# A windowed-attention and token-MLP kernel: gate factors spread on VectorE, two independent last evictions, layer norm on two engines, and a new plan

## The chip, the core and the metric

The kernel runs on one core of one Trainium2 chip. A core has TensorE (matmul), VectorE (DVE in the profile), ScalarE (ACT), GpSimd (POOL) and SyncE (SP), which here only issues DMAs. Each engine works through its own list of instructions in order, and semaphores tie the lists together. The metric is the device time of one launch in microseconds (us); lower is better.

## What is computed

```python
x = A_x                                   # 1 x 2048 x 512, bf16
g = sigmoid((x * gate_w).sum(-1))         # one gate per token
# a: 32 heads of 16, causal, each query sees its last 256 keys
q, k, v = split_heads(x @ wqkv)
p = softmax(where(0 <= i - j < 256, q @ k.T * 16**-0.5, -1e9))
a = (p @ v) @ wo
# b: an MLP over the 2048 tokens, for each of the 512 columns
h = layernorm(x)                          # over the 512 columns
u = gelu(einsum("sd,sf->df", h, w1) + b1)     # f = 1376
b = einsum("df,fs->sd", u, w2) + b2
out = g * a + (1 - g) * b
```

## The kernel before

Tokens lie in 16 tiles of 128, and in four blocks of four tiles. Everything stays in SBUF; x, the weights and the output pass DRAM once.

**Start.** x arrives in tiles `xo`; two blocks are transposed on TensorE (L702) and two by transposing DMAs (L579) into `XT`. While x and the weights arrive, TensorE does projections (L740): keys to `KT`, queries to `QZ` (L794, each query once with the even and once with the odd heads zeroed), values to `VA`, each followed by an eviction from PSUM by VectorE or ScalarE. SP's queue takes the loads in order of priority; the copies `VS` of the values with swapped halves (L774, L775) go through it too.

**Attention** goes by groups of queries that lie half a tile off the token tiles. For each group there are score matmuls (L985, and L965 for the two half tiles at the window's ends), exponentials on ScalarE (L1010, two of 128x1024 each), masks on VectorE (L1026, L1043) or GpSimd (L639), and value matmuls (L1069). VectorE then transposes 32x32 blocks, takes the reciprocal of the sum, multiplies (L1131 to L1148) and transposes back into `xo` (L1166). In L1139 the reciprocal is multiplied by exp(x . gate_w), which lies in `EZ`.

**The gate.** TensorE makes x . gate_w as a column, one token per partition (L841); VectorE limits it (L854), ScalarE takes the exponential into `ez` (L860). At L1139, though, tokens lie 32 to a partition group: `EZ` must hold in every one of the four groups of 32 partitions the factors of all four. So GpSimd splits the fp32 factor into three bf16 parts (four instructions, L866 to L869), TensorE multiplies them by four 0/1 matrices `spread` (twelve matmuls of 4 columns, L876), and VectorE or ScalarE copies the 128x16 result from PSUM to `EZ` (L885). This happens four times, once for a block.

**Layer norm.** VectorE makes the statistics (L810, L814), GpSimd one over the root of the variance (L820, L821), VectorE the normalised tile `h` (L826, 16 of them).

**The MLP.** Eleven chains u of 16 matmuls over the tokens (L740, `h` times w1 in `wb`), each waiting for all 16 tiles of `h` and for its column group of w1 (three groups, loaded in four pieces each); after the last u one gelu on ScalarE. Then w2 is loaded over w1, and 16 chains y of 15 matmuls follow, 11 from the MLP and 4 from the attention with `wo`; the bank of each is evicted by VectorE (L551) or ScalarE (L548) as c1 * y + c2 into `ot`, which is stored. The last tile is evicted in two halves of 256 columns, `f15.0` and `f15.256`, and stored once.

**The order.** `arrange` is a planner inside the program. Every task names its engine or engines with a cost, what it depends on, and a priority, which is a base from `ORDER` plus an offset by name from `SHIFT`. The planner builds the lists of all engines: the next task is one that can start earliest; among those that can start within `patience` of each other the lowest priority wins. For TensorE a change between dense matmuls (mode "d") and the tiled ones of attention adds `stick` to the priority, a change between two attention modes adds `join`. A task with two engines is offered to both. `two=True` marks VectorE instructions that share an SBUF port with GpSimd; the planner keeps those apart from GpSimd's work, and a wait is put in where a GpSimd task follows within 1 us. `Task` objects are then emitted in the planned order. For PSUM, whose tiles alias, the program itself adds a wait for whoever used the bank before, if that was another engine: readers too.

```python
pw = add(f"pow{i}", {"POOL": 1.6}, power, ag + [k0], 5)
hready.append(add(f"h{t_}", {"DVE": 0.41}, emit_h, [pw], ORDER["ln"] - 0.5 + i, two=True))
...
b, t = chain(f"u{fc}", mms, dw1[g] + hready, ORDER["u"] + ORDER["u_step"] * fc, "u")
...
gready = add("gates", {"DVE": 0.45}, gates, eready + [k3, m1[4]], 30, two=True)
```

## Time and profile before

| | |
|---|---|
| median of 3 runs | 216.52 us (214.58 to 216.78) |
| the profiled execution | 215.1 us, its span 213.4 us |
| TensorE busy | 203.0 us, 95% of the span, 3723 matmuls |
| ScalarE, VectorE, GpSimd busy | 169.0, 154.1, 56.8 us |
| matmuls of the spread, L876 | 48, in groups of 12 at 25.4, in 30 to 35 (two), and at 75.2 us |
| h tiles, L826 | 16 on VectorE, 16.1 to 57.7 us, 406 ns each |
| first matmul on h | 57.9 us |
| last matmul ends | 209.4 us |
| granted TensorE clock | 1.00 throughout |

The span goes from the first to the last instruction; the time of the execution has 1.7 us more around it. The profile's "busy" of TensorE counts modelled ends of pipelined matmuls, so 100% busy means that no gap shows, not that the array does its peak. In the chain that ended last each piece is what released the next one; a piece of TensorE with x12 stands for twelve matmuls in a row.

### The profile page before, as it was taken

The numbers are of one execution on the slowest core, as the hardware profiler recorded it, in microseconds if no ns is written. First come the engines' busy times: TensorE is split into PE (matmuls) and PEld (weight loads), VectorE is DVE, ScalarE is ACT, GpSimd is POOL, SyncE is SP. The second block draws the span as 40 slices with busy tenths as digits, with TensorE's granted clock in tenths as the row PEclk, the third lists the DMA queues.
The fourth block names the chain that finished last, engine by engine and source line by source line (L and its number), as shares of the span: only waits on it lengthen the run. The fifth ranks groups of instructions, "written<-read, shape, count | busy, mean of one in ns | idle before, by whom it ended". The sixth has DMA issues, their size and how long they took to land.

```text
span 213.4 us, 8309 instructions
## 1 busy us (share of the span) xinstructions
PE 203.0 (95%) x3723; PEld 93.6 (44%) x3723; DVE 154.1 (72%) x248; ACT 169.0 (79%) x196; POOL 56.8 (27%) x78
## 2 busy tenths in 40 slices
PE   7999998988999999999999999999999999999992
PEld 3444433432444454544554345453354445345550
DVE  1786899999988757675766768377666778537872
ACT  3164899989999789979787999778989697987721
POOL 8720422495029722021222240202230202003000
PEclk9999999999999999999999999999999999999999
DMA  4999976955330000000190693010110010000002
GB/s 145 333 181 79 281 242 198 303 199 135 82 82 3 3 3 3 3 3 0 29 367 6 213 394 78 5 54 0 59 35 3 28 49 28 28 25 28 31 3 74
DMA packets 24867, 20.34 MB, mean 95 GB/s; under 512 B 8864, under 2 KB 23200, under 8 KB 24832
## 3 DMA queue, kind: packets, MB, share of 16 engines
q1 hardware_dynamic: 21328, 19.80, 30.7%
q0 software_dynamic: 3504, 0.01, 3.0%
q8 instruction: 29, 0.48, 1.0%
q14 instruction: 6, 0.05, 0.1%
HBM read 15.47 MB, written 2.10 MB: 82 GB/s over the span
## 4 chain that ended last, share of the span: by engine, by line
PE 81%; ACT 8%; DVE 6%; DMA 2%; issue 1%; SPq 1%; ACTq 0%; DVEq 0%
PE pb L740 58%; PE ps L1069 11%; PE ps L985 8%; ACT et L1010 5%; PE ps L965 2%; DMA wqkv<-in_A_wqkv_dram 2%; DVE QZ L794 1%; DVE h L826 1%; ACT VA L693 1%; ACT KT L693 1%; DVE VA L694 1%; PE pb L841 1%; DVE ps L1131 1%; ACT XT L1010 1%; DVE XT L1026 1%
## 5 line engine op out<-in xcount | busy, mean ns | idle before, releaser
L1010 ACT ACTIVATE et<-ps 128x1024 bf16<-128x1024 f32 (+1 forms) x108 | 101.6, 1002 | 15.0 <-PE ps L985 11.4
L1010 ACT ACTIVATE XT<-ps 128x1024 bf16<-128x1024 f32 (+1 forms) x46 | 43.7, 1004 | 7.3 <-PE ps L985 3.8
L639 POOL TENSOR_SCALAR_AFFINE_SELECT et<-et 128x1024 bf16<-128x1024 bf16 (+1 forms) x26 | 30.2, 1162 | 64.6 <-ACT et L1010 45.6
L740 PEld LDWEIGHTS <-wb 128*128 128x128 bf16 (+2 forms) x352 | 30.8, 99 | 37.3 <-issue 6.0
L740 PE MATMUL pb<-h,wb 128*128 128x512 bf16 (+1 forms) x176 | 43.4, 381 | 0.0
L740 PE MATMUL pb<-ug,wb 128*128 128x512 bf16 (+1 forms) x176 | 42.8, 380 | 0.0
L740 PE MATMUL pb<-XT,wqkv 128*128 128x512 bf16 x128 | 32.3, 380 | 1.0 <-DMA wqkv<-in_A_wqkv_dram 0.4
L1131 DVE STREAM_TRANSPOSE ps<-ps 128x1024 f32<-128x1024 f32 (+1 forms) x17 | 20.4, 1197 | 8.0 <-PE ps L1069 7.9
L985 PE MATMUL ps<-QZ,KT 32*128 32x256 bf16 (+1 forms) x528 | 24.0, 262 | 2.1 <-ACT XT L1010 0.7
L1069 PEld LDWEIGHTS <-VA 128*32 128x32 bf16 (+1 forms) x1472 | 21.8, 94 | 9.6 <-issue 5.0
L639 POOL TENSOR_SCALAR_AFFINE_SELECT XT<-XT 128x1024 bf16<-128x1024 bf16 x9 | 10.3, 1145 | 56.1 <-ACT XT L1010 38.3
L794 DVE TENSOR_TENSOR QZ<-pb,par 128x1024 bf16<-128x1024 f32 x16 | 19.4, 1218 | 3.8 <-PE pb L740 3.6
L1043 DVE TENSOR_TENSOR et<-et,mask 128x1024 bf16<-128x1024 bf16 (+1 forms) x20 | 15.3, 764 | 9.2 <-ACT et L1010 9.1
L1069 PE MATMUL ps<-et,VA 128*32 128x128 bf16 (+2 forms) x1024 | 20.2, 211 | 0.0
L985 PEld LDWEIGHTS <-KT 32*128 32x128 bf16 x528 | 8.0, 92 | 24.7 <-ACT et L1010 11.2
L551 DVE TENSOR_SCALAR ot<-pb,c,c 128x512 bf16<-128x512 f32 (+1 forms) x14 | 11.0, 787 | 9.4 <-PE pb L740 9.4
L740 PE MATMUL pb<-wqkv,XT 128*128 128x512 bf16 x64 | 16.7, 381 | 0.9 <-ACT VA L693 0.5
L740 PE MATMUL pb<-wo,xo 128*128 128x512 bf16 x64 | 17.0, 380 | 0.0
L740 PEld LDWEIGHTS <-wqkv 128*128 128x128 bf16 x128 | 10.7, 97 | 14.2 <-ACT VA L693 1.2
L1166 DVE STREAM_TRANSPOSE xo<-zt 128x512 bf16<-128x512 bf16 (+1 forms) x17 | 11.5, 678 | 0.4
L550 DVE TENSOR_SCALAR ug<-pb,b1c 128x512 bf16<-128x512 f32 (+1 forms) x10 | 7.5, 751 | 5.7 <-PE pb L740 5.7
L1148 DVE TENSOR_TENSOR zt<-ps,rd 128x512 bf16<-128x512 f32 (+1 forms) x17 | 11.2, 657 | 0.5
(70 smaller groups left out, 178.9 us busy)
## 6 DMA issues: line engine op xcount, KB each, us to landing
wb<-in_B_w_dram SPq DMA_DIRECT2D x8, 512.0 KB, 6.6
wb<-in_B_w_dram SPq DMA_DIRECT2D x2, 2048.0 KB, 8.6
out_dram<-ot SPq DMA_DIRECT2D x16, 128.0 KB, 1.7
xo<-in_A_x_dram SPq DMA_DIRECT2D x3, 512.0 KB, 6.6
wb<-in_B_w_dram SPq DMA_DIRECT2D x4, 352.0 KB, 5.1
VS<-VA SPq DMA_DIRECT2D x32, 36.0 KB, 3.0
wqkv<-in_A_wqkv_dram SPq DMA_DIRECT2D x4, 256.0 KB, 5.2
wb<-in_B_w_dram SPq DMA_DIRECT2D x1, 1024.0 KB, 6.4
```

The costliest lines, as they stand in the source:

```text
L550: return nc.vector.tensor_scalar(out=out_, in0=in_, scalar1=bias, scalar2=None, op0=ALU.add)
L551: return nc.vector.tensor_scalar(out=out_, in0=in_, scalar1=scale, scalar2=bias, op0=ALU.mult, op1=ALU.add)
L639: return nc.gpsimd.affine_select(out=out_, in_=in_, pattern=[[0, n] for n in pattern] + [[step, HB]], compare_op=op, fill=0.0, base=base_, ...
L740: nc.tensor.matmul(buf(b)[:rows, :], lhsT=lhsT, rhs=rhs, start=(j == 0), stop=(j == n - 1))
L794: lambda k=k, b=b: nc.vector.tensor_tensor(out=QZ[:, k, :, (i % NQ) * SB:(i % NQ + 1) * SB], in0=buf(b)[:, None, :].to_broadcast([P, 2, SB ...
L985: made.append(nc.tensor.matmul(to[:, :, done:done + m], lhsT=keys(t_, k)[rows], rhs=q[rows], start=True, stop=True, tile_position=(32 * r, 0),
L1010: lambda n_=n_: nc.scalar.activation(out=shape(buf(e)[:, n_ * 1024:(n_ + 1) * 1024]), in_=shape(buf(b2[n_])), func=ACT.Exp, scale=SCALE),
L1043: return nc.vector.tensor_tensor(out=view, in0=view, in1=mask[:, "AB".index(x), None, :].to_broadcast([P, n_, HB]), op=ALU.mult)
L1069: return lambda: nc.tensor.matmul(to(), lhsT=v, rhs=buf(e)[rows, col:col + n], start=first, stop=last, tile_position=(rows.start, 32 * r), ...
L1131: f"n1{j}", {"DVE": 0.10 + 0.53 * f_}, lambda: nc.vector.transpose(out=view(), in_=view()), [last], 1, uses=[o],
L1148: lambda: nc.vector.tensor_tensor(out=buf(zt)[:, 0:w].rearrange("q (k b d) -> q k b d", k=4, d=DH), in0=blocks_of()[:, :, :, 0:DH], in1=bu ...
L1166: return nc.vector.transpose(out=to, in_=src)
```

## The change

Four things, and a new plan:

- The spread of the gate factors goes from GpSimd, TensorE and an eviction to VectorE alone: seven `tensor_copy` a block in fp32, four of 32x4 that bring the four partition groups of `ez` into the first group of `EZ`, and three of 32x16 that copy the first group to the others. `spread`, `z3`, `zr`, the sixteen GpSimd instructions, the 48 matmuls and the PSUM bank they used go.
- The evictions of y are marked `reads=True`. A task so marked waits for those who wrote the bank, and no longer for another such reader on another engine. It matters where two evictions read one bank, that is for the last tile.
- `h` can be made on GpSimd as well; the planner chooses.
- `lead`, `patience`, `stick`, `join`, `aside` and all offsets in `SHIFT` are new, so the order on every engine and in SP's queue is new.

```diff
 
 class Task:
     def __init__(self, name, engines, emit, deps=(), prio=50.0, lat=None, takes=(), uses=(), after=(), mode="d",
-                 two=False, ins=0):
+                 two=False, ins=0, reads=False):
         self.name = name
         self.engines = dict(engines)
         self.emit = emit
...
         self.two = two
 
         self.ins = ins
+
+        self.reads = reads
         self.takes = list(takes)
         self.uses = list(uses)
         for b in self.takes + self.uses:
...
 ORDER = dict(
     k=250.875, q=17.921, v=613.443, u=80.631, u_step=68.7, y=341.56, a=-49.601, pv=-51.223, s=-4.599,
-    gate=15.0, lead=-0.617, block=245.251, patience=0.326, m=-229.1, ln=1183.669, ev=255.775,
-    gelu=0.0, w1=71.797, pt=-57.398, stick=4.2, join=-164.3, aside=0.479, vs=2.0, wv=0.547, x=10.235,
+    gate=15.0, lead=-19.522, block=245.251, patience=0.215, m=-229.1, ln=1183.669, ev=255.775,
+    gelu=0.0, w1=71.797, pt=-57.398, stick=-171.7, join=-1591.5, aside=0.438, vs=2.0, wv=0.547, x=10.235,
     x_step=0.571, xt=11.397, xt_step=8.828,
 )
 BANKS = dict(
...
 ]
 
 SHIFT = {
...
-    "x1.4": -1901.8, "x2.8": -2292.5, "x3.12": -735.1, "xt2": -1707.8, "xt3": 662.4, "w1_00": -427.5,
...
-    "pow0": -18.0, "h0": -1266.0, "h1": -2653.7, "h2": -3891.3, "h3": -1642.6, "bs4": -1278.3, "ba4": -1289.3,
...
-    "h12": -1329.9, "h13": -1997.3, "h14": -1889.7, "h15": -1409.0, "gate0": -372.7, "gatem0": -1479.4,
...
-    "y15.10": 3400.9, "y15.11": 3855.9, "y15.13": 3855.8, "f15.0": -2180.0, "f15.256": -824.9, "o15": -1228.7,
...
+    "wv": -2289.8, "x1.4": -2247.8, "x2.8": -1082.1, "x3.12": 964.7, "xt2": -312.8, "xt3": 2434.4, "w1_00": 1746.3,
...
+    "h0": 546.5, "h1": 546.9, "h2": 627.3, "h3": 533.1, "bs4": -3903.9, "ba4": -151.4, "bs5": -4513.9,
...
+    "ba14": 528.7, "bs15": 416.3, "ba15": 389.6, "pow3": 2073.8, "h12": 818.2, "h13": -231.1, "h14": 3402.0,
...
+    "y15.13": 7360.2, "f15.0": -2153.2, "f15.256": -1705.3, "o15": 5622.7,
...
 }
...
     ez = sb.tile([P, NT], FP32, name="ez")
 
     EZ = sb.tile([P, 4 * NT], FP32, name="EZ")
-    z3 = sb.tile([P, 3, NT], BF16, name="z3")
-    zr = sb.tile([P, NT], FP32, name="zr")
     zeros = ug[:, 0, :]
     ident = sb.tile([P, P], BF16, name="ident")
-    spread = sb.tile([P, 4, P], BF16, name="spread")
     mask = sb.tile([P, 6, HB], BF16, name="mask")
     par = sb.tile([P, 2], FP32, name="par")
     gwc = sb.tile([P, 4], BF16, name="gwc")
...
         nc.gpsimd.memset(VA[:, :, H * DV:], 1.0)
 
     k5 = add("ones", {"POOL": 2.8}, ones, prio=3)
-
-    k7 = add(
-        "spread", {"ACT": 0.62},
-        lambda: nc.scalar.activation(
-            spread[:].rearrange("p a (r m) -> p a r m", r=4),
-            ident[:].rearrange("p (a m) -> p a m", m=32)[:, :, None, :].to_broadcast([P, 4, 4, 32]), ACT.Copy,
-        ),
-        [k1], prio=4,
-    )
 
     add("table", {"ACT": 1.4}, lambda: nc.scalar.activation(th[:], eps[:, 0:1], ACT.Exp), [k0], prio=0)
...
         pw = add(f"pow{i}", {"POOL": 1.6}, power, ag + [k0], 5)
         for t_ in range(4 * i, 4 * i + 4):
             def emit_h(t_=t_):
-                return nc.vector.tensor_scalar(
+                return (nc.vector if engine[0] == "DVE" else nc.gpsimd).tensor_scalar(
                     out=h[:, t_, :], in0=xo[:, t_, :], scalar1=mv[:, t_, 0:1], scalar2=rstd[:, t_:t_ + 1],
                     op0=ALU.subtract, op1=ALU.mult,
                 )
-            hready.append(add(f"h{t_}", {"DVE": 0.41}, emit_h, [pw], ORDER["ln"] - 0.5 + i, two=True))
+            hready.append(add(f"h{t_}", {"DVE": 0.41, "POOL": 0.8}, emit_h, [pw], ORDER["ln"] - 0.5 + i, two=True))
...
         )
         eready.append(ge)
 
-        def thirds(ts=ts):
-
-            nc.gpsimd.tensor_copy(out=z3[:, 0, ts], in_=ez[:, ts])
-            nc.gpsimd.tensor_tensor(out=zr[:, ts], in0=ez[:, ts], in1=z3[:, 0, ts], op=ALU.subtract)
-            nc.gpsimd.tensor_copy(out=z3[:, 1, ts], in_=zr[:, ts])
-            nc.gpsimd.tensor_tensor(out=z3[:, 2, ts], in0=zr[:, ts], in1=z3[:, 1, ts], op=ALU.subtract)
-
-        gs = add(f"third{i}", {"POOL": 3.7}, thirds, [ge], 3)
-        zb = bank("xt")
-
-        def pick(zb=zb, ts=ts):
-            return [
-                nc.tensor.matmul(
-                    buf(zb)[:, 4 * a:4 * a + 4], lhsT=spread[:, a, :], rhs=z3[:, m, ts], start=(m == 0), stop=(m == 2),
-                )
-                for a in range(4) for m in range(3)
-            ]
-
-        zp = add(f"pick{i}", {"PE": 0.35}, pick, [gs, k7], 3, takes=[zb], ins=24)
-        zready.append(add(
-            f"picked{i}", {"DVE": 0.2, "ACT": 0.25},
-            lambda zb=zb, i=i: (nc.scalar.copy if engine[0] == "ACT" else nc.vector.tensor_copy)(
-                out=EZ[:, 16 * i:16 * i + 16].rearrange("p (t a) -> p a t", a=4),
-                in_=buf(zb)[:, 0:16].rearrange("p (a t) -> p a t", t=4),
-            ),
-            [zp], 3, uses=[zb],
-        ))
+        def emit_spread(ts=ts, i=i):
+
+            to = EZ[:, 16 * i:16 * i + 16].rearrange("p (t a) -> p a t", a=4)
+            made = [nc.vector.tensor_copy(out=to[0:32, a], in_=ez[32 * a:32 * a + 32, ts]) for a in range(4)]
+            for r in range(1, 4):
+                made.append(nc.vector.tensor_copy(
+                    out=EZ[32 * r:32 * r + 32, 16 * i:16 * i + 16], in_=EZ[0:32, 16 * i:16 * i + 16]
+                ))
+            return made
+
+        zready.append(add(f"ez{i}", {"DVE": 0.9}, emit_spread, [ge], 3))
...
                 lambda b=b, ot=ot, t_=t_, c0=c0, c1_=c1_: affine(
                     buf(ot)[:, c0:c1_], buf(b)[:, c0:c1_], c1[:, t_:t_ + 1], c2[:, t_:t_ + 1]
                 ),
-                [t, gready], 2, takes=[] if c0 else [ot], uses=[b, ot] if c0 else [b],
+                [t, gready], 2, takes=[] if c0 else [ot], uses=[b, ot] if c0 else [b], reads=True,
             )
             for c0, c1_ in cols
         ]
...
                 if b.ring is not ps:
                     continue
                 for i in range(b.index, b.index + b.size):
-                    for who, ins in last[i]:
-                        if who != t.engine:
+                    for who, ins, reads in last[i]:
+                        if who != t.engine and not (reads and t.reads):
                             tc.add_manual_dep(
                                 first, ins.name,
                                 mybir.DependencyInfo(mybir.DependencyClass.Sync, mybir.DependencyReason.DATA),
                                 reason="psum bank",
                             )
-                    last[i] = [(t.engine, final)]
+                    last[i] = (last[i] if t.reads else []) + [(t.engine, final, t.reads)]
```

## The prediction

> **What bounds the kernel now.** I read the page's first part, then busy time by stretches, the chain that ended last, and the timeline at the places the change touches. The first line is busy time by engine. The others are stretches: limits, length, then busy us and (instructions) of PE, PEld, DVE, ACT, POOL, then granted clock, DMA share, GB/s.
>
> ```profile
> PE 203.0 (95%) x3723; PEld 93.6 (44%) x3723; DVE 154.1 (72%) x248; ACT 169.0 (79%) x196; POOL 56.8 (27%) x78
> ...
> 20.00:30.00 10.00, 9.76 (x110) 4.26 (x107) 8.50 (x17) 7.51 (x14) 3.42 (x13) 1.00 0.97 283
> 30.00:40.00 10.00, 8.69 (x211) 3.80 (x212) 9.49 (x20) 9.96 (x16) 3.39 (x3) 1.00 0.67 194
> 40.00:50.00 10.00, 8.72 (x153) 3.55 (x152) 9.54 (x22) 9.27 (x13) 6.84 (x10) 1.00 0.64 204
> 50.00:57.90 7.90, 7.15 (x200) 2.94 (x198) 7.51 (x18) 7.89 (x10) 1.31 (x2) 1.00 0.48 105
> 57.90:209.40 151.50, 150.87 (x2964) 70.44 (x2956) 106.91 (x149) 125.83 (x133) 32.01 (x31) 1.00 0.17 57
> ```
>
> Two regimes. From 57.9, where the first u matmul starts, to 209.4 TensorE idles 0.63 us of 151.5: only less TensorE work shortens that. From 20 to 57.9 it idles 0.24 + 1.31 + 1.28 + 0.75 = 3.58 us, while VectorE is busy 35.0 of 37.9 us and ScalarE 34.6: these two hold TensorE back, and TensorE has nothing else to do, as every u chain waits for all sixteen h tiles. The clock is full throughout.
>
> Four pieces of the chain (start, length):
>
> ```profile
> 25.45 0.45 PE pb L876 x12
> ...
> 75.07 0.28 PE pb L876 x12
> ...
> 209.43 0.56 DVE ot L551
> 210.01 0.56 ACT ot L548
> ```
>
> and from the timeline of VectorE and GpSimd:
>
> ```profile
> 21.19 0.16 DVE L854 TENSOR_SCALAR ez<-pb 128x4 f32<-128x4 f32 x1 [0.61 <-PE pb L841]
> 21.27 0.40 DVE L826 TENSOR_SCALAR h<-xo,mv,rstd 128x512 bf16<-128x512 bf16 x1
> ...
> 50.35 1.99 DVE L826 TENSOR_SCALAR h<-xo,mv,rstd 128x512 bf16<-128x512 bf16 x6
> ...
> 55.71 2.02 DVE L826 TENSOR_SCALAR h<-xo,mv,rstd 128x512 bf16<-128x512 bf16 x6
> ...
> 66.29 1.62 DVE L1043 TENSOR_TENSOR et<-et,mask 128x1024 bf16<-128x1024 bf16 x1
> ...
> 74.55 0.17 DVE L1214 TENSOR_SCALAR c<-ez 128x16 f32<-128x16 f32 x1
> 74.75 0.25 DVE L1215 RECIPROCAL c<-c 128x16 f32<-128x16 f32 x1
> 75.03 0.18 DVE L1216 TENSOR_TENSOR c<-c,b2c 128x16 f32<-128x16 f32 x1
> ...
> 0.80 2.28 POOL L663 MEMSET VA<- 128x512 bf16 x1 [0.29 <-POOLq L1304]
> ...
> 49.02 1.15 POOL L639 TENSOR_SCALAR_AFFINE_SELECT et<-et 128x1024 bf16<-128x1024 bf16 x1 [0.22 <-ACT et L1010]
> ```
>
> **The tail.** The two halves of the last tile run one after the other, 0.54 us on VectorE, then 0.56 us on ScalarE, with the last matmul done at 209.4. Without the wait both start there and the store leaves after the longer one: 210.57 becomes about 210.02, so **-0.55 us**, all on the path. What comes late next is the store, unchanged. Bounds: 0 (both halves on one engine) and -0.55. The Trainium skill speaks against this edit ("PSUM — Partial Sum Buffer", section "PSUM bank collisions raise a hardware error"): two engines that read one bank and quadrant at once collide, also at disjoint columns, and nothing is stalled. The trace shows no such overlap; by the rule the time would still fall by 0.55 and the data would be in danger, by the trace alone it falls by 0.55.
>
> **The gate spread, what goes.** 48 matmuls in four groups. Three (0.45 us each, from 25.4 to 33) lie where ScalarE and VectorE bind, and save nothing by themselves. The fourth at 75.07 lies in the full stage: 0.28, plus the break it makes in a dense run. A break costs about 0.1: in the chain two L740 matmuls take 0.54 and twelve 2.70, so 0.216 each and 0.11 over. I take **-0.38**; bounds -0.28 and -0.38. On ScalarE two copies of 0.20 go at 27 and 34, on VectorE one of 0.19 at 32; the 0.63 us at 3.83 lies in ScalarE's idle time. GpSimd loses sixteen small instructions, hidden.
>
> **The gate spread, what comes.** Seven dependent or neighbouring VectorE copies a group, 4 or 16 elements wide. No row shows a copy from one partition group to another. Below: 0.08 us from start to start, as from L854 to the next instruction, 0.56 for seven. Above: 0.28, as from L1215 to L1216, 2.0 for seven. The nearest row is L1214 with 0.17, so 1.2 for seven. Three groups fall before 57.9: 3.6 us on a full VectorE (1.7 to 6.0). The fourth falls where VectorE idles 45 us, and costs nothing; its factors are first used dozens of us later. The skill ("VectorE: DVE Perf Modes", section "Two Vector instructions with no wait between them") has a rule against it: an instruction whose start quadrant differs from the one before is held until that is done, so seven would take seven whole durations, 1.2 by L1214's row; without it, 0.6. What queues behind the copies is VectorE's in-order list, evictions for which TensorE and ScalarE wait.
>
> **h on GpSimd.** The new offsets of h are -231 to 3402 (before -3891 to -1266), so it yields to nearly everything, and goes where an engine is idle: GpSimd, 15 us busy of 37.9. An h costs VectorE 0.33 (1.99 / 6). If all fifteen after 20 us go, VectorE gets 5.0 us back; if none, 0. Its price on GpSimd no row shows: half a select is 0.57 (1024 elements take 1.15), the scattered memset of 512 elements 2.28. The select is nearer, contiguous bf16 in and out; I take 0.65. Behind each h wait the next h and GpSimd's selects. At 66.29 a mask multiply took 1.62 instead of 0.69 while GpSimd worked through five selects: up to 0.93 us for each collision.
>
> **Together, 20 to 57.9.** VectorE: -5.0 - 0.2 + 3.6 = -1.6; ScalarE -0.4. Evictions go to either, so 2.0 us shared by two is **-1.0**. The last twelve h, now two bursts from 50.35 to 57.7 with evictions between, run beside VectorE, so u starts 2 to 3 us sooner and fills most of the 0.75 idle there: **-0.5**. Both come out of the 3.58 idle. Ends: 0 and -3.58; and a loss, priced below.
>
> **The replan.** All else moves too. SP's queue: by the new priorities the last quarter of x (x3.12) is 16th of the loads, before 13th; what is ahead of it is 5.85 MB instead of 6.25, so by bytes it leaves at about 30.6 instead of 32.7 (an estimate from its issue time). The transposed load xt2 goes from 10th to 14th, behind 4.85 MB, so to about 25.4, and lands 8.2 us later at 34; the copies of its keys stood at 43 and later. Most of w1 still follows x3.12; none of that should hold u. In the full stage the order can win the 0.63 idle, and change the number of breaks: 61 dense runs lie in the chain, ten more or fewer are 1.1 us either way. I take **-0.3**, half the idle.
>
> **Sum.** -0.55 - 0.38 - 1.0 - 0.5 - 0.3 = -2.7 us. The profiled execution took 215.1 (span 213.4 and 1.7 around it): 212.4. The median, 216.52, stands 1.4 above that execution; with the same distance the median is **213.8**, -1.3%. The three runs lie 2.2 us apart, so 1% (2.17 us: 214.35 and 218.69) is about what can be told from no change.
>
> **Rivals.** (1) *The order gains nothing*: VectorE gets back less than the copies take, or breaks eat the rest. Only tail and fourth group stay, -0.9, 215.6. For it: 95% busy VectorE, and an upper price of 2.0 a group, 6.0 in all, more than the 5.0 that h gives back. Against: h can leave. Probability 0.28, the cases within 1%. (2) *Slower: u waits for h on GpSimd.* All u chains need the last h. If twelve are left after 48.8, when rstd is done, and each takes a whole select's time, 1.15, the last ends at 62.6, 4.7 us later than now. The 176 u matmuls take 176 x 0.216 = 38 of the 66 us from 57.9 to 123.9, so 0.58 of TensorE's time stands empty in that wait: +2.7, with the 0.9 saved +1.8, so 218.3; at 1.4 us each 221. It decides as soon as the last h ends after 59.5 (0.9 / 0.58 = 1.6 us later). For it: 2.28 for a memset, the stretched multiply, the low priority of h. Against: GpSimd idles, and eight of the h can be made before x3.12 lands. Probability 0.22 that this or a bad order makes it slower by over 1%. (3) *Larger gain*: all 3.58 and 0.63 filled, ten breaks fewer: -0.9 - 4.2 - 1.1 = -6.2, 210.3. Probability 0.17 for more than 3.6 us. (4) *It doesn't do what it says*: h stays on VectorE, both last halves on one engine; then -0.4 + 1.7 (3.4 net on VectorE, halved): 217.8, in the cases of (1). The forecast, -2.2 to -3.6: 0.33.
>
> Faster by over 1% is 0.33 + 0.17 = 0.50, within 1% 0.28, slower 0.22. The range goes from the floor of (3), 210.2, to a little beyond (2), 219.0; the forecast alone gives 212.9 to 214.3.
>
> **What would show it.** Both ot halves start within 0.1 us of the last matmul; no L876 group; seven EZ copies of about 0.17 each; h on GpSimd at 0.6 to 0.7; the first matmul that reads h at 55 rather than 57.9; under 2.2 us of TensorE idle from 20 to there; some 61 dense runs after. Wrong if h costs GpSimd over 1 us, if u starts after 59, if the copies take over 2 us a group, or if there are many more dense runs.

## The result, and the profile after

The changed kernel takes 225.26 us (median of 4 runs, 224.84 to 225.84) against 216.21 us for the kernel before (median of 4, 214.58 to 216.78): a ratio of 1.043, 95% interval 1.037 to 1.050. It is slower by 9 us, where 213.8 was forecast and 219.0 was the upper end of the range. The profiled execution took 224.84 us with a span of 223.1, so 9.7 us of span have to be found. Ratios and intervals, here and below, leave out the few executions of a kernel that took over 1.5% longer than its fastest; medians keep them, so the two can differ by some tenths of a per cent.

The page of the changed kernel: busy time by engine, the granted clock in 40 slices of 5.6 us, and the group of instructions that makes `h` on GpSimd.

```profile
PE 197.8 (89%) x3639; PEld 92.6 (41%) x3675; DVE 159.1 (71%) x258; ACT 164.7 (74%) x187; POOL 91.5 (41%) x83
...
PEclk9999969995999999999999999999999999999999
...
L815 POOL TENSOR_SCALAR h<-xo,mv,rstd 128x512 bf16<-128x512 bf16 x15 | 31.4, 2098 | 0.1
```

Fifteen of the sixteen h stand on GpSimd, at 2.10 us each in the mean (least 2.07); the forecast had 0.65, the planner inside the program 0.8. GpSimd's busy time went from 56.8 to 91.5 us. The trace lacks some 36 of the changed kernel's matmul records, so I compare starts and ends rather than counts.

Busy time by stretches (columns as in the prediction); the last two rows run from the first matmul on h to the end of the last matmul:

```profile
20.00:30.00 10.00, 6.27 (x90) 2.87 (x90) 9.41 (x17) 7.50 (x12) 4.42 (x5) 0.95 0.82 208
30.00:40.00 10.00, 8.84 (x145) 3.41 (x152) 8.24 (x20) 8.98 (x14) 9.77 (x8) 0.88 1.21 331
40.00:50.00 10.00, 6.54 (x137) 2.84 (x131) 9.69 (x25) 7.87 (x11) 9.92 (x8) 0.97 0.20 43
50.00:60.00 10.00, 6.37 (x105) 2.92 (x107) 4.40 (x7) 3.62 (x5) 9.92 (x9) 0.69 0.06 13
...
62.90:75.00 12.10, 9.54 (x214) 4.54 (x212) 11.65 (x19) 8.17 (x11) 7.47 (x6) 1.00 0.35 83
75.00:219.10 144.10, 139.93 (x2830) 66.74 (x2856) 100.82 (x140) 117.35 (x122) 29.80 (x26) 1.00 0.17 58
```

From 30 to 60 GpSimd, the fifth column, is busy for 29.6 of 30 us: it is the engine that binds there. From 20 to 60 TensorE stands still for some 12.0 us (40 less 28.0; waits with a named cause make 10.7 of them) where it stood for 3.6 before. Its granted clock, 1.00 throughout before, falls as low as 0.69 in a stretch. Closer in, it is halved twice:

```profile
28.98:32.38 3.40, 2.76 (x31) 0.89 (x30) 2.19 (x5) 2.99 (x6) 2.38 (x3) 0.50 1.03 363
49.46:56.27 6.81, 2.79 (x53) 1.34 (x53) 1.70 (x3) 0.31 (x1) 6.81 (x6) 0.50 0.01 2
```

TensorE was busy for 5.55 us in these two stretches; at full clock that work takes half, so 2.8 us is an estimate of what the clock cost. VectorE and ScalarE, which were to be relieved, are busy for only 4.4 and 3.6 of the 10 us from 50 to 60: they wait too. The first matmul that reads h moves from 57.9 to 62.9 (+5.0), and the last matmul ends at 219.1 instead of 209.4. So 5.0 of the 9.7 us are lost before that matmul. The other 4.7 come after it, where attention left undone has to be made up: TensorE was busy for 48.3 us before its first matmul on h, in the kernel before for 52.2.

The chain that ended last, at the place where the time goes:

```profile
45.80 6.19 POOL h L815 x3
51.99 1.11 POOL et L637
53.14 0.96 PE ps L1042 x39
```

and from the waits (who waited for whom: total, times, longest):

```profile
PE ps L1042 <- POOL et L637: 7.4, 2, 5.5
...
ACT ot L546 <- DVE ot L549: 7.9, 1, 7.9
```

Three h in a row, 6.2 us, then a mask of attention (L637) that had been queued behind them on GpSimd, then the value matmuls that need the mask; in one of the two cases TensorE waited 5.5 us. The last h ends at 65.9, after the first matmuls on the earlier tiles have started. The second wait is the tail: ScalarE's half of the last tile still waits for VectorE's (7.9 us is all of ScalarE's idle time there; only its last 0.6 lies behind the last matmul). In the chain the halves follow each other as before:

```profile
219.11 0.55 DVE ot L549
...
219.69 0.56 ACT ot L546
```

Last, the copies that spread the gate factors, and GpSimd beside them, from the timelines of VectorE and GpSimd:

```profile
22.09 1.65 DVE L856 COPY EZ<-ez 32x4 f32<-32x4 f32 x4
23.77 1.50 DVE L858 COPY EZ<-EZ 32x16 f32<-32x16 f32 x3
...
22.04 1.16 POOL L637 TENSOR_SCALAR_AFFINE_SELECT et<-et 128x1024 bf16<-128x1024 bf16 x1 [1.22 <-ACT et L983]
24.10 1.15 POOL L637 TENSOR_SCALAR_AFFINE_SELECT et<-et 128x1024 bf16<-128x1024 bf16 x1 [0.90 <-ACT et L983]
```

Undisturbed, a copy takes 0.16 us. Here the first of the four takes 1.13 and the last of the three 1.15: each began beside a mask on GpSimd and ended with it. The four groups take 3.15, 1.87, 1.87 and 4.36 us, 11.25 in all, where 4.8 was reckoned.

### The profile page after: what moved, and what is told of

Read it like the earlier page. It is cut to its first block, busy times and chain, and to the rows that moved or that the text cites. A ratio compares the mean times of both kernels' runs of the same rounds, so it can differ in the third digit from the quotient of the medians.

```text
span 223.1 us, 8196 instructions
## 1 busy us (share of the span) xinstructions
PE 197.8 (89%) x3639; PEld 92.6 (41%) x3675; DVE 159.1 (71%) x258; ACT 164.7 (74%) x187; POOL 91.5 (41%) x83
## 4 chain that ended last, share of the span: by engine, by line
PE 72%; POOL 9%; DVE 7%; issue 4%; DMA 3%; ACT 2%; SPq 1%; POOLq 0%
PE pb L729 52%; PE ps L1042 10%; PE ps L958 7%; POOL h L815 6%; DMA wqkv<-in_A_wqkv_dram 3%; PE ps L938 2%; POOL et L637 2%; DVE EZ L858 2%; DVE QZ L783 2%; DVE EZ L856 2%; ACT et L983 1%; SPq L569 1%; DVE ps L1104 1%; POOL XT L637 1%; POOL rstd L810 0%
## 5 line engine op out<-in xcount | busy, mean ns | idle before, releaser
L983 ACT ACTIVATE et<-ps 128x1024 bf16<-128x1024 f32 (+1 forms) x106 | 99.4, 991 | 18.8 <-PE ps L958 12.9
L637 POOL TENSOR_SCALAR_AFFINE_SELECT et<-et 128x1024 bf16<-128x1024 bf16 (+1 forms) x32 | 36.6, 1147 | 98.5 <-ACT et L983 78.7
L983 ACT ACTIVATE XT<-ps 128x1024 bf16<-128x1024 f32 x48 | 46.6, 1024 | 10.0 <-PE ps L958 9.5
L729 PE MATMUL pb<-ug,wb 128*128 128x512 bf16 (+1 forms) x164 | 41.3, 380 | 1.9 <-issue 1.8
L729 PE MATMUL pb<-h,wb 128*128 128x512 bf16 (+1 forms) x167 | 41.2, 380 | 1.3 <-issue 1.3
L815 POOL TENSOR_SCALAR h<-xo,mv,rstd 128x512 bf16<-128x512 bf16 x15 | 31.4, 2098 | 0.1
L1016 DVE TENSOR_TENSOR et<-et,mask 128x1024 bf16<-128x1024 bf16 (+1 forms) x16 | 11.6, 724 | 12.1 <-ACT et L983 12.1
L637 POOL TENSOR_SCALAR_AFFINE_SELECT XT<-XT 128x1024 bf16<-128x1024 bf16 x9 | 10.3, 1145 | 21.3 <-ACT XT L983 18.6
L549 DVE TENSOR_SCALAR ot<-pb,c,c 128x512 bf16<-128x512 f32 (+1 forms) x16 | 12.7, 792 | 7.3 <-PE pb L729 7.0
L999 DVE TENSOR_TENSOR XT<-XT,mask 128x2048 bf16<-128x2048 bf16 x8 | 9.9, 1232 | 6.3 <-ACT XT L983 6.3
L682 ACT ACTIVATE KT<-pb 128x512 bf16<-128x512 f32 x10 | 6.0, 601 | 9.5 <-PE pb L729 9.5
```

The costliest lines, as they stand in the source:

```text
L549: return nc.vector.tensor_scalar(out=out_, in0=in_, scalar1=scale, scalar2=bias, op0=ALU.mult, op1=ALU.add)
L637: return nc.gpsimd.affine_select(out=out_, in_=in_, pattern=[[0, n] for n in pattern] + [[step, HB]], compare_op=op, fill=0.0, base=base_, ...
L682: return nc.scalar.activation(out_(), in_(), ACT.Copy)
L729: nc.tensor.matmul(buf(b)[:rows, :], lhsT=lhsT, rhs=rhs, start=(j == 0), stop=(j == n - 1))
L815: return (nc.vector if engine[0] == "DVE" else nc.gpsimd).tensor_scalar(out=h[:, t_, :], in0=xo[:, t_, :], scalar1=mv[:, t_, 0:1], scalar2 ...
L983: lambda n_=n_: nc.scalar.activation(out=shape(buf(e)[:, n_ * 1024:(n_ + 1) * 1024]), in_=shape(buf(b2[n_])), func=ACT.Exp, scale=SCALE),
```

## The experiments

The theory formed from this: **(T1)** h at 2.07 us on GpSimd makes GpSimd the bound from 30 to 60 us, holds up the masks behind it and the last h, and TensorE pays with idle time and clock. Its rivals: **(T2)** the VectorE copies cost it, and **(T3)** the new order does, whatever stands on GpSimd. "Before" is run again on the same chip in each comparison. The runs at a glance:

| run | us | ratio to before, interval | first matmul on h | TensorE busy, 20 to 60 |
|---|---|---|---|---|
| before | 215.6 to 216.2 | 1 | 57.9 | 36.4 |
| after | 225.26 | 1.043 (1.037 to 1.050) | 62.9 | 28.0 |
| a_h_dve | 217.99 | 1.0067 (1.0024 to 1.0111) | 59.2 | 33.7 |
| a_masks_dve | 223.31, one run | | 62.8 | 31.9 |
| a_ez_act | 224.18, one run | | 62.8 | 29.8 |
| b_copies | 221.92 | 1.0221 (1.0146 to 1.0297) | 62.8 | 34.0 |
| b_copies_late | 219.80 | 1.0186 (1.0110 to 1.0262) | 59.3 | 33.7 |
| b_late_pad | 218.53 | 1.0137 (1.0095 to 1.0180) | 60.5 | 33.7 |
| a_h_late | 215.59 | 0.9984 (0.9942 to 1.0025) | 56.0 | 35.3 |
| a_h03_late | 217.97 | 1.0109 (1.0074 to 1.0145) | 56.2 | 34.4 |
| a_mend | 217.25 | 1.0057 (1.0015 to 1.0099) | 56.1 | 34.5 |
| b_tail2 | 215.65 | 0.9977 (0.9947 to 1.0008) | 58.0 | 36.4 |
| a_h_late_tail2 | 215.90 | 0.9998 (0.9970 to 1.0027) | 54.4 | 35.6 |
| b_probe | 215.41, one run | | | |
| b_probe2 | 220.71, one run | | | |

### h back on VectorE, in the new order

```diff
-                return (nc.vector if engine[0] == "DVE" else nc.gpsimd).tensor_scalar(
+                return nc.vector.tensor_scalar(
...
```

The wait that the program puts before an h on GpSimd goes with it.

> The changed kernel with its order of all engines kept, but the 15 h tiles that were on GpSimd are emitted on VectorE at the same places of the order. Theory 1 (an h costs GpSimd 2.07 us where the plan has 0.8, so masks and u chains come late): GpSimd loses 31 us of work, VectorE gains 15 x 0.33 = 5.0 us, the 9.7 us of span come back but for what VectorE's 5 us cost: 213 to 217 us. Theory 2 (the copies of the gate factors hold VectorE, 11.3 us in all): the copies stay, VectorE is fuller still: 220 us or more. Theory 3 (the new order is worse by itself, whatever h costs): 220 us or more, with TensorE's idle time spread over the span.

Measured 217.99: **7.3 of the 9 us come back by this edit alone**, every other part of the change still being there. That is T1; the 7.3 us include what h on GpSimd did to its neighbours, masks and copies among them. What is left, 0.67%, belongs to the copies or to the order.

### Only the masks off GpSimd; only the copies off VectorE

Ten masks planned on GpSimd from 30 to 58 us are made there by VectorE in the first; the 28 copies are made by ScalarE in the second.

```diff
-            engine[0] = t.engine
+            engine[0] = "DVE" if t.name in MOVED else t.engine     # first: ten masks
...
-            made = [nc.vector.tensor_copy(out=to[0:32, a], ...
+            made = [nc.scalar.copy(out=to[0:32, a], ...            # second: all 28 copies
```

> The changed kernel with h on GpSimd as planned, but the ten masks that GpSimd is planned to make between 30 and 58 us of the plan (m0.A1 to m3.A1) on VectorE. If the loss comes through masks that queue behind h on GpSimd, and the value matmuls behind them, the 5.5 us wait of TensorE at 47.6 goes and the time falls to 217 to 221. If it comes through the u chains that wait for the last h, the first u matmul stays at 60 or later and the time at 222 to 226. Theory 2: VectorE is fuller by 7 us, so slower than 225.

> The changed kernel with the 28 copies of the gate factors on ScalarE instead of VectorE, at the same places of the order; h stays on GpSimd. Theory 1: 223 to 226, since h is untouched. Theory 2 (VectorE held by copies that take up to 1.1 us while GpSimd works): VectorE gets 11 us back, 220 or less.

With the masks gone the 5.5 us wait is gone, and yet only 2 us come back, in a single run and with the masks now VectorE's. The trace of the first run says why: h on GpSimd alone lasts nearly as long (the last begins at 60.6 and ends at 62.7), and the first matmul on h starts at 62.8.

```profile
L729 PE MATMUL pb<-h,wb x176: 379/379/417, 62.8 to 132.6; 128*128 128x512 bf16 x160, 128*96 128x512 bf16 x16
L815 POOL TENSOR_SCALAR h<-xo,mv,rstd x15: 2068/2080/2598, 12.8 to 60.6; 128x512 bf16<-128x512 bf16 x15
```

So the masks were the wait that showed, and h the length that stayed: the second of the two outcomes expected. The copies on ScalarE took 0.20 us each, not stretched, and gave 1.1 us back in a single run. Neither is the main cause.

### The copies alone, in the old order

The kernel before, with the spread by seven VectorE copies a block at the place of the old eviction; the 48 matmuls, GpSimd's parts and the evictions go. h stays on VectorE.

```diff
-            lambda zb=zb, i=i: (nc.scalar.copy if engine[0] == "ACT" else nc.vector.tensor_copy)(...),
+            emit_spread,     # the seven tensor_copy of the changed kernel
```

> The kernel before, order kept, with the gate factors spread by the seven VectorE copies where the copy from PSUM was; the split on GpSimd, the 48 matmuls and the spread matrices are left out. h stays on VectorE. The prediction's prices: -0.38 for the fourth group, and 3.6 us of VectorE shared by two engines at most +1.7 before 57.9: 215.5 to 218. Theory 1: copies at 0.17 each and no stretch, since GpSimd is mostly idle: within 1% of before. Theory 2: slower than before by 2 us or more.

Measured 221.92, +2.2%: beyond both the prediction's 215.5 to 218 and T1's 1%, so **in the old order the copies do cost**, as T2 says. VectorE's timeline:

```profile
31.88 1.19 DVE L788 TENSOR_TENSOR QZ<-pb,par 128x1024 bf16<-128x1024 f32 x1
32.99 0.67 DVE L870 COPY EZ<-ez 32x4 f32<-32x4 f32 x4
33.69 0.52 DVE L872 COPY EZ<-EZ 32x16 f32<-32x16 f32 x3
34.24 0.69 DVE L688 CAST KT<-pb 128x512 bf16<-128x512 f32 x1
```

A group takes 0.67 + 0.52 and little between, 1.23 us, nearly the 1.2 forecast; but all of it comes before the next eviction (KT), for which TensorE waits. Busy time by stretches of the same run:

```profile
30.00:40.00 10.00, 6.67 (x88) 1.77 (x84) 9.66 (x27) 6.67 (x10) 1.15 (x1) 0.74 0.70 194
34.85:41.66 6.81, 6.42 (x59) 1.75 (x60) 6.57 (x20) 3.58 (x5) 2.29 (x2) 0.50 0.92 259
40.00:50.00 10.00, 8.79 (x220) 3.96 (x220) 8.83 (x22) 8.57 (x12) 5.50 (x7) 0.92 0.56 185
```

TensorE idles 3.3 of the 10 us from 30, 1.9 of them in one wait for that eviction, and then its clock is halved from 34.85 to 41.66. It was busy for 6.42 us there, so an estimate of the clock's cost is 3.2 us: in this run the copies are paid once as delay and once more as clock.

### The same, with three groups held late, without and with padding

The copies of groups 2 to 4 are emitted just before the attention group that first needs them. In the second run, twelve small matmuls that nobody reads stand where the spreading matmuls stood.

```diff
+        held_ez = {f"picked{i}": f"n1{4 * i - 1}" for i in range(1, NSB)}   # held until just before n13, n17, n111
...
+            return [nc.tensor.matmul(buf(zb)[:, 4 * a:4 * a + 4], lhsT=ident[:], rhs=ident[:, 0:4], ...)   # padding
```

> The order of the kernel before, layer norm on VectorE, the gate factors spread by seven VectorE copies a group as in the kernel after; the copies of the first group where they stood, those of the other three held back until just before the first attention group that reads them, where the matmuls of stage u already fill TensorE and VectorE is busy for about 70 of 100 us. Theory 1 (a copy costs its full time only where VectorE sets the pace, that is before the first matmul of stage u): only the first group's 1.2 us is left on the path, and the single look's 219.9 us of span with early copies falls to 214.5 to 215.5, a median of 216.5 to 217.7 beside about 216.1. Rival 2 (the copies cost wherever they stand, by the reads of quarters of the partitions or by a wait for them): 220 to 222, as with early copies. Rival 3 (the gain of the removed matmuls, GpSimd steps and ScalarE evictions shows once the copies are hidden): under 215.5.

> The kernel before with the gate factors spread by VectorE copies, those of the last three groups held late (219.8 us as run before), and with twelve small matmuls per group of which nothing is read at the place where the twelve spreading matmuls stood, so that TensorE's list of instructions is as long as in the kernel before at every point. In the run without them TensorE stood still for 1.24, 0.78, 0.88 and 1.05 us (3.95 us in all) for nothing that the profile shows, and such a gap followed a block of TensorE's instructions being loaded; the kernel before has one such gap of 0.50 us. Theory 1 (those gaps belong to where the blocks of the instruction list begin, not to the copies): the gaps go, 216.0 to 217.3 us, the first group's copies (1.2 us) and the late copies that stand in the chain being all that is left. Rival 2 (the time is the copies' own, wherever they stand): 219.5 to 220.5, with the extra matmuls' 0.45 us a group on top of what they were.

Measured 219.80 and 218.53: both between the theories. The chain of the first:

```profile
57.48 0.61 PE ps L1061 x64
58.09 1.24 issue
59.33 1.47 PE pb L734 x6
...
70.87 0.61 DVE EZ L870
...
71.50 1.09 DVE EZ L870
```

Two things are to be seen. The late group at 70.87 stands directly in front of its reader and is again stretched beside a mask on GpSimd (1.09 for one copy): "late" was too late, and that group is on the path a second time. And TensorE pauses for 1.24 us at 58.09 for nothing that the profile shows; three more such pauses of 0.78 to 1.05 follow. In the padded run the pause at 58 is gone, but that execution has one of 2.40 at 43.73, and the kernel before, with six added GpSimd instructions near its end, one of 1.28 at 42.43 (and in the second such probe one of 2.38 at 42.89), though TensorE's work there is that of before, where no such pause shows. A block of instructions was loaded in the three us ahead of each of these pauses, but there are 28 such loads in the first run, most of them with no pause. That they cause the pauses isn't shown, and the intervals of the two runs overlap, so how much of the 5.8 us that the copies alone cost in the old order is copies and how much such pauses stays open.

### The new order with neither

h on VectorE and copies 2 to 4 late, in the new order; then the same with the first four h on GpSimd (12 to 20 us, when it has nothing else to do); then that with the last tile evicted whole.

```diff
-                return (nc.vector if engine[0] == "DVE" else nc.gpsimd).tensor_scalar(
+                return nc.vector.tensor_scalar(                                                     # a_h_late
+                return (nc.vector if engine[0] == "DVE" or t_ > 3 else nc.gpsimd).tensor_scalar(    # a_h03_late, a_mend
...
+                lambda b=b, ot=ot, t_=t_, c0=c0, c1_=c1_: None if c0 else affine(buf(ot), buf(b), ...)   # a_mend
```

> The changed kernel in its own order, the whole layer norm on VectorE, the copies of groups 2 to 4 late. Against the same with early copies (217.99): theory 1 (three groups of copies cost 1.2 us each where VectorE is full, 9.2 to 9.9 of 10 us between 20 and 70 us) 214.5 to 216.0, the first matmul on the layer norm's result at 56 to 58 us instead of 59.2. Rival 2 (this order has already put the copies in gaps): 217.5 to 218.5. Beside the run above it tells what four tiles on GpSimd bring: by theory 1, at 0.41 us of VectorE each, up to 1.6 us if VectorE is full while they run, nothing if the loads of x set the pace there.

> The changed kernel with late copies, the first four tiles of the layer norm on GpSimd and twelve on VectorE, the last tile evicted in two halves as in the changed kernel: against the run with the last tile evicted whole (217.25) and the one with no tile on GpSimd (215.59). Theory 1 (four tiles of 2.07 us at 12 to 21 us cost by themselves, since the first masks wait behind them, 4.1 us of wait in the earlier run, and TensorE, busy for 6.4 of the 10 us from 20 to 30 and then at a granted clock of 0.84, pays for it): 217.0 to 218.0. Rival 2 (the whole eviction of the last tile made that run slow): 215.3 to 216.0.

> The changed kernel in its own order, but only the first four tiles of the layer norm on GpSimd (12 to 21 us, when it has nothing else to do), the other twelve on VectorE, the copies of groups 2 to 4 late as in the run above, and the last tile evicted whole by one engine. Theory 1 (the time went to 11 tiles of 2.07 us on GpSimd, to the masks behind them and to early copies on a full VectorE): the first matmul on the layer norm's result comes before 58 us and the median lies at 214.5 to 216.5. Rival 2 (the new order of the work is itself worse than the old, whatever stands on GpSimd): 217.5 to 219, no better than with the whole layer norm on VectorE (217.99). Rival 3 (four tiles on GpSimd delay what VectorE does beside them, by copies stretched to 1.1 us): 218 to 221.

215.59, 217.97, 217.25. The first is level with the kernel before, and late copies are worth 0.8% in it: 1.8 us by the ratios (1.0067 and 0.9984), 2.4 by the medians (217.99 and 215.59).

What the order does by itself shows only where all else is alike. With late copies and h on VectorE in both, the old order took 219.80 (1.0186) and the new one 215.59 (0.9984); with early copies 221.92 (1.0221) and 217.99 (1.0067). So T3 falls: **the new order is the better one for these copies, by 3 to 4 us**, which about wins back what they cost in the old order, and the two together end level with the kernel before. Part of the difference may be unexplained pauses: with late copies the chain of the old order has four, 3.95 us in all, that of the new one 1.01 and 0.50.

Against 215.59 the other two lose 1.7 to 2.4 us, with four h on an idle GpSimd. The version with the whole eviction (217.25, run first) was expected at 214.5 to 216.5; that the four h alone lose was forecast only after it, and the reason given was wrong: the masks at 21.85 and 23.91 wait for ScalarE, not for h. The traces show something else, the first group of copies. Without h on GpSimd (a_h_late):

```profile
23.97 1.48 DVE L856 COPY EZ<-ez 32x4 f32<-32x4 f32 x4
25.48 0.53 DVE L858 COPY EZ<-EZ 32x16 f32<-32x16 f32 x3
...
20.00:30.00 10.00, 7.67 (x97) 3.29 (x94) 9.54 (x21) 8.22 (x13) 3.45 (x3) 1.00 0.74 192
30.00:40.00 10.00, 8.71 (x144) 3.42 (x144) 8.89 (x21) 8.97 (x16) 6.63 (x8) 1.00 1.08 363
```

then with four (a_h03_late):

```profile
21.90 1.65 DVE L856 COPY EZ<-ez 32x4 f32<-32x4 f32 x4
23.59 1.50 DVE L858 COPY EZ<-EZ 32x16 f32<-32x16 f32 x3
...
20.00:30.00 10.00, 6.53 (x87) 2.71 (x84) 9.51 (x18) 7.49 (x13) 4.18 (x5) 0.95 0.75 199
30.00:40.00 10.00, 8.90 (x136) 3.31 (x134) 8.01 (x19) 8.37 (x12) 6.21 (x8) 0.87 1.20 331
```

VectorE comes to the copies 2.1 us sooner, but now they meet the masks of 21.85 and 23.91 where they met one, take 3.15 us instead of 2.01, and end only 0.9 us sooner. TensorE idles 3.5 instead of 2.3 us from 20 to 30 and then runs at 0.87. The first matmul on h comes at 56.2 against 56.0: what four h on GpSimd spare VectorE buys nothing there. The executions on record go with the clock: those of a_h_late took 214.29 to 215.04 us with a mean granted clock of 0.995 or more, and 216.14 or more with 0.988 to 0.992; all seven of a_h03_late had 0.982 to 0.992. That the clock makes the difference of the medians fits this, but no run changes the clock alone.

### The tail, with two banks

The last tile's fifteen matmuls become thirty of 256 columns, whose halves lie in two different banks of PSUM.

```diff
+                    if name == f"y{NT - 1}":
+                        made.append(nc.tensor.matmul(buf(b)[:rows, 0:256], lhsT=lhsT, rhs=rhs[:, 0:256], ...))
+                        made.append(nc.tensor.matmul(singles[twin[0]][:rows, 256:512], lhsT=lhsT, rhs=rhs[:, 256:512], ...))
```

> The kernel before, with the last output tile accumulated in two banks of PSUM, columns 0 to 255 in one and 256 to 511 in the other (thirty matmuls of 256 columns in place of fifteen of 512), each half evicted by its own engine as now. Theory 1 (what orders the two last evictions is that they read one bank): both start together, the 0.54 and 0.56 us that now follow each other lie side by side, and the end comes 0.5 to 0.6 us sooner after the last matmul, 215.4 to 215.8 us beside about 216.0 if the split matmuls cost nothing. Rival 2 (the order comes from the output tile that both write, or from VectorE's count): ScalarE's eviction again starts only when VectorE's has ended, no change. Rival 3 (more matmuls cost more than the tail gains): ends together, yet the time is the same or up to 1 us longer.

> The changed kernel with the whole layer norm on VectorE and the copies of the last three groups late (215.59 us as run before, beside 215.61 for the kernel before), and its last tile in two banks as in the run above. Theory 1 (the two evictions go side by side once the banks differ): 0.5 to 0.6 us less, 214.9 to 215.3, a ratio of about 0.996 to the kernel before. Rival 2 (they still follow each other, or the split matmuls take the gain): 215.4 to 216.0. A gain of over 1% over the kernel before is expected by neither.

The timeline of the first, VectorE and ScalarE:

```profile
209.30 0.54 DVE L553 TENSOR_SCALAR ot<-pb,c,c 128x256 bf16<-128x256 f32 x1 [0.59 <-PE pb L747]
...
209.30 0.56 ACT L550 ACTIVATE ot<-pb,c,c 128x256 bf16<-128x256 f32 x1 [1.57 <-PE pb L747]
```

Now both start in the same 10 ns, each released by TensorE. From the last matmul's end (209.26) to the end of the last eviction it is 0.60 us, where it was 1.17 before (209.40 to 210.57). So it is the shared bank that orders them: the change drops the program's own wait, but as long as both halves lie in one bank ScalarE still waits for VectorE, as the changed kernel shows; the wait must come from behind the program, and from where was not traced. The gain, 0.57 us or 0.26%, isn't measurable in either kernel: 0.9977 (0.9947 to 1.0008), and 0.9998 where the same kernel with one bank had 0.9984, so there the rival's range (215.4 to 216.0) holds. No version here beats the kernel before by more than its interval.

### What a GpSimd instruction costs

The kernel before, with added instructions on GpSimd after its last mask.

```diff
+            if t.name == 'm14.B1':
+                g.tensor_scalar(out=scr[:], in0=h[:, 0, :], scalar1=mv[:, 0, 0:1], scalar2=rstd[:, 0:1], op0=ALU.subtract, op1=ALU.mult)
...
```

> The kernel before with six more GpSimd instructions after its last mask (about 196 us), whose results are not used: the layer norm's tensor_scalar with two scalars read per partition on 512 columns, the same on 256 columns, one with a single scalar read per partition, one with two constants, a copy, and a product of two tensors, each on 512 columns in bfloat16. Theory 1 (the price on GpSimd is by the element and grows with what is read per element): 2.07 us for the first, about half on 256 columns, less for one scalar and for constants; Rival 2 (a fixed price of the form, such as its start): about the same on 256 columns as on 512. Forecast of the others by the share that scalar reads would have: 1.2 to 1.6 us with one scalar, 0.6 to 1.2 with constants or a copy. The time of the kernel: unchanged within 1%, since GpSimd has nothing to do there.

> The kernel before with six more GpSimd instructions after its last mask, written to tiles of the layer norm that nobody reads any more: the layer norm's tensor_scalar with two scalars read per partition on 64, 512, 1024 and 2048 columns, a copy of 2048 columns, and a product of four tiles with a factor per partition and tile given as a tensor (2048 columns). In the earlier probe 512 columns took 2.08 us and 256 took 2.00. Theory 1 (nearly all of it is a price per instruction): about 1.9 us on 64 columns, 2.1 on 512, 2.2 to 2.3 on 1024, 2.5 to 2.8 on 2048, so a plan that gives GpSimd few long instructions would pay far less. Rival 2 (a price by the element above some width): over 4 us on 1024 and over 8 on 2048. The copy: 1.5 to 4 us; the product: 2 to 5 us for four tiles, against 8.3 for four tiles by tensor_scalar.

The first run's timeline of GpSimd (two scalars per partition on 512 and on 256 columns, one on 512, two constants, a copy, a product):

```profile
195.54 2.08 POOL L1272 TENSOR_SCALAR scr<-h,mv,rstd 128x512 bf16<-128x512 bf16 x1
197.72 2.00 POOL L1273 TENSOR_SCALAR scr<-h,mv,rstd 128x256 bf16<-128x256 bf16 x1
199.81 2.26 POOL L1274 TENSOR_SCALAR scr<-h,mv 128x512 bf16<-128x512 bf16 x1
202.17 1.93 POOL L1275 TENSOR_SCALAR scr<-h 128x512 bf16<-128x512 bf16 x1
204.16 0.95 POOL L1276 COPY scr<-h 128x512 bf16<-128x512 bf16 x1
205.19 1.16 POOL L1277 TENSOR_TENSOR scr<-h 128x512 bf16<-128x512 bf16 x1
```

and the second's chain, the first form on 64, 512, 1024 and 2048 columns:

```profile
198.08 0.59 POOL h L1272
...
198.76 2.08 POOL h L1272
...
200.93 3.90 POOL h L1272
...
204.92 7.25 POOL h L1272
```

The price is **by the element**: 0.59, 2.08, 3.90, 7.25 us are about 0.4 us and 3.3 ns a column, four times the 0.8 ns a column of VectorE (0.407 us for 512). The rival of the second run had that, with 4 and 8 us as its marks a little too high; the guess between the two runs, a price per instruction, is refuted. It rested on the 2.00 us for 256 columns, which should be 1.2 by this line; VectorE was then making masks of 1.23 us at 197.40 and 199.41, so a collision may have lengthened it, which was not tested (the one-scalar form began beside such a mask too; in the changed kernel the longest h, 2.49 us, did). Scalars read per partition make little of it: constants take 1.93, where 0.6 to 1.2 was expected. A plain copy of 512 takes 0.95, of 2048 1.89. In the second run the added instructions are themselves what ends last (GpSimd is done at 217.8), so its 220.71 us say nothing else.

## Why the prediction was wrong

**The step that failed: "h on GpSimd", 0.65 us each.** The working had both rows, 0.57 from half a select and 2.28 from the memset, and took the first, since it is contiguous bf16 in and out. Measured: 2.07 in the kernel, 2.08 alone. The select is a different operation with its own rate (1.15 for 1024 columns, so 1.1 ns a column); the same engine takes 0.6 ns a column for a copy and 3.3 for this form. Contiguity was the wrong likeness; nothing in the trace of before showed a `tensor_scalar` of this size on GpSimd, so the two bounds were all one had, and the far one was the nearer to the truth. Worth: 7.3 us, where -0.5 and the 5.0 us of relief stood.

**The rival was named right and priced too low.** "u waits for h on GpSimd" is what happened: its point of decision was a last h after 59.5, and it came at 65.9. But it was priced at 1.15 and 1.4 us each, 218.3 and 221 (a slip: by its own formula 1.4 gives 220.1), and the range was cut at 219.0, though the working's own upper price, 2.28, gives 76.2 for the last h and 226.2 by that formula. A bound that has been written down must go into the range. The formula was too low as well: a last h at 65.9, 8.0 us later than 57.9, gives 0.58 x 8.0 - 0.9 = +3.7, so 220.3, and 225.26 was measured. It counts only TensorE's empty time in front of u. It leaves out the masks behind h, which the working had named as queued there (5.5 us in one wait), and the clock (2.8 us, the estimate above). And u didn't wait for all sixteen tiles: its first matmul ran at 62.9, before the last h was done.

**"Shared by two is -1.0" failed.** The copies' price was right where nothing runs beside them, 1.23 us a group against 1.2, each copy beginning when the one before had ended. But a sum of busy time, halved for two engines, missed where they stand: in the old order, kept as it was, a group stands before the next eviction, for which TensorE waits, and in the new order three early groups cost 1.8 to 2.4 us where a net relief was reckoned. ScalarE took no load over in the changed kernel: 187 instructions against 196. There the copies took up to 4.36 us a group beside GpSimd; the prediction had seen the stretched multiply (1.62 for 0.69) and not laid that on the copies.

**The tail, -0.55: the mechanism is right, the edit doesn't make it.** The change alters nothing there; two banks do. The prediction had doubted the safety of the overlap and not that it would come.

**The replan, -0.3, was mis-sized:** it was taken as half of 0.63 us of idle time. With the copies in place the new order is worth 3 to 4 us against the old one, which only wins back what the copies cost there: with h on VectorE and late copies the sum of both is 0.9984 (0.9942 to 1.0025). u then starts 1.9 us sooner (56.0), and from there to the last matmul it takes 155.1 us instead of 151.5, since less was done before (48.4 us of TensorE's work instead of 52.2). The **fourth group's -0.38** was not measured by itself.

In steps: 215.6 for the new order with late copies and h on VectorE, +2.4 for early copies, +7.3 for h on GpSimd: 225.3, the time after. That this adds up shows nothing, since each step is the difference of two medians in the row; what it shows is the shares.

Of the signs named ahead, "h costs GpSimd over 1 us", "u starts after 59" and, in two of four groups (3.15 and 4.36), "the copies take over 2 us a group" came; the ot halves did not start together, and TensorE idled far more than 2.2 us.

## What to carry to other kernels

Before work goes to an idle engine, find that engine's own time for that very form of instruction; where the trace has none, run it beside a stage where the engine idles, and until then let the range reach the worst row. Price what is queued behind the moved work on the new engine, and what runs on its neighbour meanwhile, before counting the relief on the old one. When parts change, compare orders with the same parts in both. Idle time of TensorE in the middle of a kernel can be paid twice, as delay and as clock: look for a halved clock behind a stop.

## What the runs showed of the hardware

- **GpSimd**, layer norm's `tensor_scalar`, bf16: about 0.4 us and 3.3 ns a column, against 0.407 us for 512 on VectorE. The Trainium skill ("GPSIMD Engine Reference", section "4.1 Engine selection") calls one-input work on GpSimd roughly line-rate; the copy (0.95 us for 512, 1.89 for 2048) fits that better than this form, which takes four times VectorE's time a column; there the measurement decides.
- **VectorE beside GpSimd**: a copy of 32x4 takes 0.16 us alone and up to 1.13 when a select is under way, ending with it (22.09 to 23.22, the select 22.04 to 23.20). The skill ("SBUF — State Buffer", section "Who interferes with whom") has the rule: the two share a port pair, and whoever comes second is blocked for the whole instruction. The rows with selects agree. Beside GpSimd's `tensor_scalar` it doesn't hold as it stands. In the changed kernel four copies ran from 39.23 to 40.16 inside an h of 38.86 to 40.93, 0.93 us instead of 0.67. In the second probe one mask multiply, begun inside the 2.08 us instruction, took its usual 1.23 us, and one beside the 7.25 us instruction took 3.54 instead of 0.68 and ended 2 us before it:

```profile
199.94 1.23 DVE L1026 TENSOR_TENSOR et<-et,mask 128x2048 bf16<-128x2048 bf16 x1
...
206.56 3.54 DVE L1026 TENSOR_TENSOR XT<-XT,mask 128x1024 bf16<-128x1024 bf16 x1
```

- **The clock**: 1.00 in every stretch of before; in the changed kernel 0.50 for 3.40 and 6.81 us, behind and during stops of TensorE of 2.3 and 5.5 us, and single matmuls took up to 634 ns instead of 379. A stop doesn't always cost clock: the padded run idled 3.2 us in this stretch, 2.40 in one pause, and kept 1.00:

```profile
40.00:50.00 10.00, 6.78 (x137) 2.85 (x138) 8.36 (x19) 7.48 (x12) 5.31 (x7) 1.00 0.59 196
```

- **Unexplained pauses of TensorE** of 0.8 to 2.4 us occur at places that change from one version to the next (58.09, 43.73, 42.43 us).
